# Output in two column halves, so that the left half of every block can be combined and stored under the last weight loads

## Chip, cores, metric

One core of one Trainium2 chip. The metric is the device time of one execution in microseconds, median of several. The trace's span is about 1.8 us shorter than the time, so spans are compared with spans and times with times.

## The reference, cut to what matters

Attention over 8 x 8 heads of 576 positions (a plain window of 32 in half of the heads, a dilated one in the other half), then a soft mixture of 8 experts with 4 slots each:

```python
x = attn_out.transpose(0, 2, 1, 3).reshape(4608, 512)
logits = x @ phi                           # (4608, 32)
d = softmax(logits, axis=0)                # dispatch: over all rows
slot_input = d.T @ x                       # needs every row
for e in range(8):
    slot_out[e] = relu(slot_input[e] @ w1[e]) @ w2[e]
c = softmax(logits, axis=1)                # combine
out = c @ slot_out                         # (4608, 512), fp32
```

An output element needs all 32 slots, so the slot outputs of all experts, so all of w2 — but only the columns of w2 that it lies in. That is what the change uses.

## The kernel before

All loads cast fp32 to fp16 on the way and are issued from POOL, as are the stores, which cast back. Weights stream in behind q, k, v through the whole kernel; w2 of experts 2, 3, 4, 6 and 7 comes last, into memory that the attention gives up.

```python
def load_w2(e, pieces=1):
    src = moe_w2[e].rearrange("(h p l) n -> p h (l n)", h=2, l=4)   # runs of 4 rows: 8 KB read, 4 KB written
    dst = w2t[e].rearrange("p (h l) n -> p h (l n)", h=2)
    if pieces == 1:
        nc.gpsimd.dma_start(out=dst, in_=src)
        return
    ...                                                             # expert 7 in four pieces
# order of the last loads: 0, 1, 5, 2, 3, 4, 6, then 7 in 4 pieces

so = psum_e.tile([128, DMODEL], FP32, name="so", tag="so")
early = [0, 1, 5, 2, 3, 4, 6]
jobs = [(e, 4 * fc + c) for fc in range(2) for e in early for c in range(4)]
jobs += [(7, c) for c in range(8)]
for i, (e, c) in enumerate(jobs):
    ...                                    # matmul: so[32a:32a+32, :] += h of expert e, times w2t[e][:, c, :]
nc.scalar.copy(out=so_sb[:, 0:256], in_=so[:, 0:256])
nc.vector.tensor_copy(out=so_sb[:, 256:512], in_=so[:, 256:512])
...
for blk in range(NFIN):                    # 36 blocks of 128 rows
    r0 = 128 * blk
    fp = psum_f.tile([128, DMODEL], FP32, name=f"f_{blk}", tag="f")
    nc.tensor.matmul(fp, ET[:, r0 : r0 + 128], so_sb, start=True, stop=True)
    ot = out_pool.tile([128, DMODEL], FP16, name=f"ot_{blk}", tag="ot")
    ...                                    # ACT and DVE in turn: ot = fp * rrow
    nc.gpsimd.dma_start(out=out[r0 : r0 + 128, :], in_=ot)
```

The softmax here doesn't subtract the row's maximum and nothing guards it: scores larger than these inputs give would overflow.

Of the kernel before, what the change touches and what calls it, by code (L numbers as in the profile page):

```python
# [9 lines left out]
FP32 = mybir.dt.float32  # L10
FP16 = mybir.dt.float16
U32 = mybir.dt.uint32
AF = mybir.ActivationFunctionType
ALU = mybir.AluOpType
# [10 lines left out]
DMODEL = H * D  # L25
# [14 lines left out]
NE = NT + DIL + 1  # L40
NFIN = N_ROWS // 128
UNITS = 7


def make_masks():
# [19 lines left out]
def kernel(  # L65
# [10 lines left out]
    nc = tc.nc  # L76
# [6 lines left out]
    consts = ctx.enter_context(tc.tile_pool(name="consts", bufs=1))  # L83
# [8 lines left out]
    ET = consts.tile([128, N_ROWS + 64], FP16, name="ET")  # L92
# [1 line left out]
    rcol = consts.tile([128, N_SLOTS], FP32, name="rcol")  # L94
    siTm = consts.tile([128, 4, E_EXP, N_SLOTS], FP16, name="siTm")
    rrow = consts.tile([128, NFIN], FP32, name="rrow")
    so_sb = consts.tile([128, DMODEL], FP16, name="so_sb")

    w1_pool = ctx.enter_context(tc.tile_pool(name="w1p", bufs=1))
    w2a_pool = ctx.enter_context(tc.tile_pool(name="w2a", bufs=1))  # L100
# [1 line left out]
    w2t = {e: w2a_pool.tile([128, 8, DMODEL], FP16, name=f"w2_{e}", tag=f"w2_{e}") for e in range(2)}  # L102
# [4 lines left out]
    QK_SLAB, V_SLAB = 2 * (32 + S + S + 80 + S + S + 16), 4096  # L107
    kTp, kTd, qTp, qTd, vP, vD, vL = [], [], [], [], [], [], []
    for i in range(2):
        slab = fix.tile([128, QK_SLAB], FP16, name=f"qk{i}", tag=f"qk{i}")  # L110
        o = 0
# [3 lines left out]
    for i in range(NV):  # L115
        slab = fix.tile([128, V_SLAB], FP16, name=f"v{i}", tag=f"v{i}")
        o = 0
# [4 lines left out]
    def slab_weights(e, tag, n):  # L122
        t = fix.tile([128, n], FP16, name=f"w2_{e}", tag=tag)
        w2t[e] = t[:, 0 : 8 * DMODEL].rearrange("p (c n) -> p c n", c=8)
# [5 lines left out]
    vs_pool = tc.alloc_tile_pool(name="vstage", bufs=2, side="right")  # L130
    raw_pool = tc.alloc_tile_pool(name="raw", bufs=2, side="right")
# [61 lines left out]
    def load_w1(e, i):  # L193
        src = moe_w1[e].rearrange("(c p) f -> p c f", p=128)
        nc.gpsimd.dma_start(out=w1t[e][:, 2 * i : 2 * i + 2, :], in_=src[:, 2 * i : 2 * i + 2, :])  # L195

    def load_w2(e, pieces=1):
        src = moe_w2[e].rearrange("(h p l) n -> p h (l n)", h=2, l=4)
        dst = w2t[e].rearrange("p (h l) n -> p h (l n)", h=2)
        if pieces == 1:  # L200
            nc.gpsimd.dma_start(out=dst, in_=src)
            return
        n = 8 * DMODEL // pieces
        for i in range(pieces):
            h, o = divmod(n * i, 4 * DMODEL)
            nc.gpsimd.dma_start(out=dst[:, h, o : o + n], in_=src[:, h, o : o + n])


    def qk_plain(ti, b):
# [69 lines left out]
    def emit_av(b, kind, i):  # L279
        u0, u1 = CHUNKS[kind][i : i + 2]  # L280
        o = psum_o.tile([128, UNITS, D + 1], FP32, name=f"o_{b}_{kind}{i}", tag="o")
        o_t[(b, kind, i)] = o
# [37 lines left out]
    def emit_norm(b, kind, i):  # L320
# [6 lines left out]
        else:  # L327
            if i == 0:
                xd_t[b] = x_pool.tile([128, DIL + 1, 4 * D], FP16, name=f"xd_{b}", tag="xd")
            x, nq = xd_t[b], 128  # L330
        rc = s_pool.tile([128, UNITS], FP32, name=f"rc_{b}_{kind}{i}", tag="rc")
        nc.vector.reciprocal(out=rc[0:nq, 0:n], in_=o[0:nq, 0:n, D])  # L332
# [127 lines left out]
    def weights(b, g):  # L460
        if b < B - 2:
            if g == 1 or b > 0:
                load_w1(*next_w1.pop(0))
        elif b == B - 2:
            if g == 0:
                while next_w1:
                    load_w1(*next_w1.pop(0))
                load_w2(0)
                load_w2(1)
            else:  # L470
                slab_weights(5, "v2", V_SLAB)
                load_w2(5)
        elif g == 0:
            nonlocal_pools["w2b"] = open_w2b()
        else:
            slab_weights(7, "v0", V_SLAB)
            load_w2(7, 4)

    nonlocal_pools = {}

    def open_w2b():
        raw_pool.release()
        vs_pool.release()
        pool = tc.alloc_tile_pool(name="w2b", bufs=1, side="right")
        for e in (2, 3, 4):
            w2t[e] = pool.tile([128, 8, DMODEL], FP16, name=f"w2_{e}", tag=f"w2_{e}")
            load_w2(e)
        slab_weights(6, "qk0", QK_SLAB)
        load_w2(6)
        return pool  # L490

    def slot0(b):
        att, b1, b2, b3 = b < B, b - 1 >= 0 and b <= B, 2 <= b < B + 2, b + 1 < B
        if att:
            qk_dil(1, b, 1)
            emit_scores(b, 0)
            if b + 2 < B:
                load_qk(0, b + 2)
                load_qk(1, b + 2)
            weights(b, 0)  # L500
# [28 lines left out]
    def slot1(b):  # L529
        att, b1, b3 = b < B, 1 <= b <= B, b + 1 < B  # L530
        if b3:
            qk_plain(0, b + 1)
        if att:
            emit_scores(b, 1)
            if b + 2 < B:
                load_v(b + 2)
            weights(b, 1)
            emit_av(b, "p", 0)
            emit_norm(b, "p", 0)
        if b1:  # L540
            back_xT_dil(b - 1, 0)
        if b3:
            qk_plain(1, b + 1)
        if att:
            emit_av(b, "p", 1)
            emit_norm(b, "p", 1)
        if b1:
            back_xT_dil(b - 1, 1)

    def slot2(b):  # L550
        att, b1, b3 = b < B, 1 <= b <= B, b + 1 < B
        if b3:
            qk_dil(0, b + 1, 0)
        if att:
            emit_scores(b, 2)
            emit_av(b, "p", 2)
            emit_norm(b, "p", 2)
        if b3:
            qk_dil(0, b + 1, 1)
        if b1:  # L560
            back_logits(b - 1, 0)
        if att:
            emit_av(b, "p", 3)
            emit_norm(b, "p", 3)
        if b3:
            qk_dil(1, b + 1, 0)
            spread_v_left(b + 1)
            shift_v_plain(b + 1)
            shift_v_left(b + 1)
        if b1:  # L570
            back_logits(b - 1, 1)

    with tc.manual_schedule(engines=None):
        prologue()
        for b in range(B + 2):
            slot0(b)
            slot1(b)
            slot2(b)
    w2b_pool = nonlocal_pools["w2b"]

    psum_o.release()
    psum_s.release()
# [2 lines left out]
    xT_pool.release()  # L585
    x_pool.release()
    h_pool = tc.alloc_tile_pool(name="hp", bufs=1)
    out_pool = tc.alloc_tile_pool(name="outp", bufs=10)


    psum_e = tc.alloc_tile_pool(name="psum_e", bufs=1, space=bass.MemoryType.PSUM)
    hTm = [h_pool.tile([128, 4, 128], FP16, name=f"hTm{g}", tag=f"hTm{g}") for g in range(4)]
    for g in range(4):
# [8 lines left out]
        out=diag,  # L602
        in0=UT[:, 0:4, :].rearrange("p c (e s) -> p c e s", e=E_EXP),
        in1=rcol.rearrange("p (e s) -> p e s", e=E_EXP)[:, None, :, :].broadcast_to(
            [128, 4, E_EXP, S_PER_E]
        ),
        op=ALU.mult,
    )
    hps = [psum_e.tile([128, 512], FP32, name=f"hps{fc}", tag=f"hps{fc}") for fc in range(2)]
    for fc in range(2):  # L610
        for g in range(2):
            for dc in range(4):
                for j in range(4):
                    e = 4 * g + j
# [4 lines left out]
                        start=(g == 0 and dc == 0),  # L619
                        stop=(g == 1 and dc == 3),  # L620
# [3 lines left out]
    for fc in range(2):  # L624
# [5 lines left out]
        for g in range(2):  # L630
            dst = hTm[2 * g + fc].rearrange("p c (j s) -> p c j s", j=4)[:, :, :, 16 * g : 16 * g + 16]
            (nc.vector.tensor_copy, nc.scalar.copy)[g](out=dst, in_=hT4[:, :, :, 16 * g : 16 * g + 16])
    rs = ring.tile([128, NFIN], FP32, name="rs", tag="ring")
    for blk in range(NFIN):
# [4 lines left out]
            start=True,  # L639
            stop=True,  # L640
        )
    nc.vector.reciprocal(out=rrow, in_=rs)
    so = psum_e.tile([128, DMODEL], FP32, name="so", tag="so")
    early = [0, 1, 5, 2, 3, 4, 6]
    jobs = [(e, 4 * fc + c) for fc in range(2) for e in early for c in range(4)]
    jobs += [(7, c) for c in range(8)]
    for i, (e, c) in enumerate(jobs):
        g, j, a = e // 4, e % 4, c % 4
        nc.tensor.matmul(  # L649
            so[32 * a : 32 * a + 32, :],  # L650
            hTm[2 * g + c // 4][:, c % 4, 32 * j : 32 * j + 32],
            w2t[e][:, c, :],
            start=(i < 4),
            stop=(i >= len(jobs) - 4),
        )
    nc.scalar.copy(out=so_sb[:, 0:256], in_=so[:, 0:256])
    nc.vector.tensor_copy(out=so_sb[:, 256:512], in_=so[:, 256:512])
    psum_e.release()


    psum_f = tc.alloc_tile_pool(name="psum_f", bufs=6, space=bass.MemoryType.PSUM)
    for blk in range(NFIN):
        r0 = 128 * blk
        fp = psum_f.tile([128, DMODEL], FP32, name=f"f_{blk}", tag="f")
        nc.tensor.matmul(fp, ET[:, r0 : r0 + 128], so_sb, start=True, stop=True)  # L665
        ot = out_pool.tile([128, DMODEL], FP16, name=f"ot_{blk}", tag="ot")
        if blk % 2 == 0:
            nc.scalar.activation(out=ot, in_=fp, func=AF.Copy, scale=rrow[:, blk : blk + 1])  # L668
        else:
            nc.vector.tensor_scalar(  # L670
                out=ot, in0=fp, scalar1=rrow[:, blk : blk + 1], scalar2=None, op0=ALU.mult
            )
        nc.gpsimd.dma_start(out=out[r0 : r0 + 128, :], in_=ot)  # L673
    psum_f.release()
    out_pool.release()
    h_pool.release()
    fix.release()
    w2b_pool.release()


# [28 lines left out]
```

## Time and profile before

| | before |
|---|---|
| time, median | 192.23 us (192.01 to 192.81) |
| span of the trace | 190.7 us |
| last w2 landing / first store landing / last store landing | 159.45 / 164.5 / 187.3 us |
| HBM read / written | 62.20 MB / 9.44 MB |

The landings are the issue times of the POOL timeline plus the landing time of each issue. The slices, the chain, the windows over the hole and the POOL timeline are shown in the prediction, which reads them.

### The profile page before, as it was taken

To read this page: it belongs to the slowest core of one execution; us is meant where nothing else is said; L and a number is where in the kernel's file an instruction comes from. 1 tells how busy PE (TensorE), PEld (TensorE's weight loads), DVE (VectorE), ACT (ScalarE), POOL (GpSimd) and SP (SyncE) were. 2 spreads that over 40 slices of the span, in tenths; PEclk is the share of its full clock that TensorE was granted. 3 is DMA by queue.
4 is the path that set the end of the run, shared out by engine and by line. 5 is a ranking of instruction groups with operands and counts; after the bars stand their busy time and mean duration, and the time that the engine had idled before them with its cause. 6 is when DMAs were issued, how large, how long until landed. Compare 5 with 4: busy or idle time off the path is not lost.

```text
span 190.7 us, 5116 instructions
## 1 busy us (share of the span) xinstructions
PE 127.4 (67%) x2224; PEld 72.1 (38%) x2224; DVE 104.5 (55%) x230; ACT 85.3 (45%) x144; POOL 96.2 (50%) x134
## 2 busy tenths in 40 slices
PE   2061058999996897894798799996960156878300
PEld 0031025757665365473357366555320022211000
DVE  3583708798999289689089794714120002756510
ACT  2031056777972764960764966540020002754500
POOL 7759762966944845834944662111100000998830
PEclk9999999999999699999589999955596558965555
DMA  5999999999999999999999999999999980999991
GB/s 122 182 181 205 189 200 194 210 197 195 214 198 197 215 195 202 210 194 203 210 195 201 211 212 214 217 211 217 215 213 218 208 161 13 303 407 407 410 405 50
DMA packets 40662, 41.00 MB, mean 215 GB/s; under 512 B 20800, under 2 KB 25536, under 8 KB 40640
## 3 DMA queue, kind: packets, MB, share of 16 engines
q0 software_dynamic: 40352, 40.41, 119.2%
q8 instruction: 17, 0.28, 0.5%
q1 hardware_dynamic: 288, 0.27, 0.5%
q14 instruction: 5, 0.04, 0.1%
HBM read 62.20 MB, written 9.44 MB: 376 GB/s over the span
## 4 chain that ended last, share of the span: by engine, by line
DMA 61%; PE 12%; issue 9%; POOL 7%; DVE 4%; ACT 3%; POOLq 0%; ACTq 0%
DMA w<-in_moe_w_dram 42%; DMA vsa<-in_v_dram 15%; DMA raw<-in_q_dram 4%; POOL out_dram L673 3%; ACT p L271 2%; PE sa L260 2%; PE sb L249 2%; PE lg L379 2%; POOL v L159 2%; DVE ot L670 2%; PE sa L249 1%; PE o_p L311 1%; PE o_d L311 1%; PE rd L360 1%; DVE qk L222 1%
## 5 line engine op out<-in xcount | busy, mean ns | idle before, releaser
L673 POOL DMA_DIRECT2D out_dram<-ot x36 | 19.0, 533 | 29.6 <-ACT ot L668 27.6
L271 ACT ACTIVATE p<-sa 128x576 f16<-128x576 f32 (+2 forms) x24 | 19.6, 818 | 20.0 <-PE sb L260 19.8
L249 PE MATMUL sa<-masks,ident 128*128 128x288 f16 (+2 forms) x48 | 14.5, 388 | 21.1 <-ACT p L271 17.6
L213 DVE STREAM_TRANSPOSE qk<-raw 128x576 uint32<-128x576 uint32 x16 | 20.0, 1250 | 8.1 <-DMA raw<-in_q_dram 6.7
L311 PEld LDWEIGHTS <-p 128*128 128x128 f16 (+2 forms) x448 | 17.5, 105 | 14.2 <-issue 9.2
L249 PEld LDWEIGHTS <-ident 128*128 128x128 f16 x96 | 9.8, 109 | 32.8 <-issue 27.3
L222 DVE STREAM_TRANSPOSE qk<-raw 128x320 uint32<-128x320 uint32 (+1 forms) x32 | 21.6, 679 | 0.3
L175 ACT COPY v<-vsa 128x1024 f16<-128x1024 f16 x8 | 8.4, 1045 | 25.2 <-DMA vsa<-in_v_dram 25.2
L271 ACT ACTIVATE p<-sb 128x576 f16<-128x576 f32 (+2 forms) x24 | 19.5, 813 | 0.0
L260 PE MATMUL sa<-qk 32*128 32x96 f16 (+2 forms) x448 | 16.1, 214 | 4.8 <-DVE qk L213 4.8
L333 DVE TENSOR_TENSOR xp<-o_p,rc_p 96x384 f16<-96x384 f32 x32 | 17.7, 554 | 1.3
L379 PE MATMUL lg<-xTd,phi 128*128 128x288 f16 x32 | 18.2, 659 | 0.0
L260 PEld LDWEIGHTS <-qk 32*128 32x128 f16 x896 | 12.5, 101 | 15.0 <-issue 9.5
L332 DVE RECIPROCAL rc_p<-o_p 96x6 f32<-96x6 f32 x32 | 5.7, 179 | 22.0 <-PE o_p L311 21.5
L670 DVE TENSOR_SCALAR ot<-f,rrow 128x512 f16<-128x512 f32 x18 | 13.1, 749 | 7.8 <-DMA out_dram<-ot 7.1
L665 PE MATMUL f<-so_sb,ET 128*128 128x512 f16 x36 | 14.8, 464 | 3.7 <-DVE ot L670 1.6
L311 PE MATMUL o_p<-v,p 128*128 128x65 f16 (+1 forms) x192 | 13.1, 211 | 5.1 <-POOL v L191 5.1
L260 PE MATMUL sb<-qk 32*128 32x96 f16 (+2 forms) x448 | 16.2, 214 | 0.0
L668 ACT ACTIVATE ot<-f,rrow 128x512 f16<-128x512 f32 x18 | 11.9, 689 | 8.7 <-PE f L665 4.8
L649 PE MATMUL so<-w,hTm 128*32 128x512 f16 x64 | 7.1, 536 | 12.8 <-DMA w<-in_moe_w_dram 12.4
L333 DVE TENSOR_TENSOR xd<-o_d,rc_d 128x448 f16<-128x448 f32 (+1 forms) x24 | 14.5, 602 | 0.8
L195 POOL DMA_DIRECT2D w<-in_moe_w_dram x16 | 11.4, 712 | 6.9 <-DMA raw<-in_k_dram 3.2
(77 smaller groups left out, 235.0 us busy)
## 6 DMA issues: line engine op xcount, KB each, us to landing
out_dram<-ot POOLq DMA_DIRECT2D x36, 256.0 KB, 4.5
w<-in_moe_w_dram POOLq DMA_DIRECT2D x16, 512.0 KB, 15.6
w<-in_moe_w_dram POOLq DMA_DIRECT2D x7, 1024.0 KB, 26.6
raw<-in_q_dram POOLq DMA_DIRECT2D x7, 576.0 KB, 12.5
raw<-in_k_dram POOLq DMA_DIRECT2D x7, 576.0 KB, 13.9
v<-in_v_dram POOLq DMA_DIRECT2D x8, 288.0 KB, 13.4
vsa<-in_v_dram POOLq DMA_DIRECT2D x8, 256.0 KB, 13.4
w<-in_moe_w_dram POOLq DMA_DIRECT2D x4, 256.0 KB, 30.9
```

Source lines behind the costliest of these rows:

```text
L213: nc.vector.transpose(out=dst, in_=src)
L222: nc.vector.transpose(out=o, in_=i)
L249: nc.tensor.matmul(sps[h // 2][:, h % 2, 0:n], ident, bias, start=True, stop=False, skip_group_check=True,)
L260: nc.tensor.matmul(sps[h // 2][:, h % 2, c0 : c0 + w], kt_[32 * h : 32 * h + 32, k0 : k0 + 128, tt], qt_[32 * h : 32 * h + 32, q0 : q0 + w ...
L271: nc.scalar.activation(out=pt, in_=sps[ab][:, :, 0:n], func=AF.Exp, scale=SCALE)
L311: nc.tensor.matmul(o[p0 : p0 + np_, n, :], l, rr, start=(k == 0), stop=(k == len(jobs) - 1), skip_group_check=True,)
L333: nc.vector.tensor_tensor(out=x.rearrange("p t (h d) -> p (t h) d", h=4)[0:nq, u0:u1, :], in0=o[0:nq, 0:n, 0:D], in1=rc[0:nq, 0:n, None].b ...
L379: nc.tensor.matmul(lp, phi4[:, kc].rearrange("p c s -> p (c s)"), rhs, start=(kc == 0), stop=(kc == 3))
L665: nc.tensor.matmul(fp, ET[:, r0 : r0 + 128], so_sb, start=True, stop=True)
L668: nc.scalar.activation(out=ot, in_=fp, func=AF.Copy, scale=rrow[:, blk : blk + 1])
L670: nc.vector.tensor_scalar(out=ot, in0=fp, scalar1=rrow[:, blk : blk + 1], scalar2=None, op0=ALU.mult)
L673: nc.gpsimd.dma_start(out=out[r0 : r0 + 128, :], in_=ot)
```

## The change

Intent: load w2 of the last four experts (3, 4, 6, 7) as left column halves first and right halves after all of those; then the left half of the slot outputs is complete while the right halves still load, and the left half of all 36 output blocks can be combined, evicted and put into the queue under those loads. Cut to its core:

```diff
-    def load_w2(e, pieces=1):
+    def load_w2(e, half=None):
...
+        src = moe_w2[e].rearrange("(h p l) n -> h p l n", h=2, l=4)
+        c0 = NH * half                                    # NH = 256
+        for h in range(2):
+            nc.gpsimd.dma_start(
+                out=w2t[e][:, 4 * h : 4 * h + 4, c0 : c0 + NH], in_=src[h][:, :, c0 : c0 + NH]
+            )
...
+            load_w2(2)
+            for e in HALVED[:3]:
+                load_w2(e, 0)
         else:
             slab_weights(7, "v0", V_SLAB)
-            load_w2(7, 4)
+            load_w2(7, 0)
+            for e in HALVED:
+                load_w2(e, 1)
+    HALVED = (3, 4, 6, 7)
...
-    for blk in range(NFIN):
+    def combine(half, pair):                              # two blocks of 128 rows, half the columns
+        fp = psum_f.tile([128, 2, NH], FP32, name=f"f{half}_{pair}", tag="f")
...
+        nc.gpsimd.dma_start(
+            out=out[r0 : r0 + 256, NH * half : NH * half + NH].rearrange("(k p) n -> p k n", k=2),
+            in_=ot,
+        )
+    with tc.manual_schedule(engines=None):
+        slot_out(0, ORDER)
+        slot_out(1, ORDER[:4])
+        at = {5: 0, 9: 1, 13: 2}
+        for pair in range(NFIN // 2):
+            combine(0, pair)
+            if pair in at:
+                slot_out(1, (HALVED[at[pair]],))
+        slot_out(1, HALVED[3:])
+        for pair in range(NFIN // 2):
+            combine(1, pair)
```

More of the change, by code (lines that the diff above doesn't have):

```diff
@@ L42 @@
 UNITS = 7
+NH = DMODEL // 2
 def make_masks():
@@ L96 @@
     rrow = consts.tile([128, NFIN], FP32, name="rrow")
-    so_sb = consts.tile([128, DMODEL], FP16, name="so_sb")
+    so_sb = [consts.tile([128, NH], FP16, name=f"so_sb{i}") for i in range(2)]
     w1_pool = ctx.enter_context(tc.tile_pool(name="w1p", bufs=1))
@@ L195, in load_w1 @@
         nc.gpsimd.dma_start(out=w1t[e][:, 2 * i : 2 * i + 2, :], in_=src[:, 2 * i : 2 * i + 2, :])
-    def load_w2(e, pieces=1):
-        src = moe_w2[e].rearrange("(h p l) n -> p h (l n)", h=2, l=4)
-        dst = w2t[e].rearrange("p (h l) n -> p h (l n)", h=2)
-        if pieces == 1:
-            nc.gpsimd.dma_start(out=dst, in_=src)
-            return
-        n = 8 * DMODEL // pieces
-        for i in range(pieces):
-            h, o = divmod(n * i, 4 * DMODEL)
-            nc.gpsimd.dma_start(out=dst[:, h, o : o + n], in_=src[:, h, o : o + n])
+    def load_w2(e, half=None):
+        if half is None:
+            nc.gpsimd.dma_start(
+                out=w2t[e].rearrange("p (h l) n -> p h (l n)", h=2),
+                in_=moe_w2[e].rearrange("(h p l) n -> p h (l n)", h=2, l=4),
+            )
+            return
+        src = moe_w2[e].rearrange("(h p l) n -> h p l n", h=2, l=4)
[4 more added lines that the diff above has]
+            )
     def qk_plain(ti, b):
@@ L473, in weights @@
         elif g == 0:
-            nonlocal_pools["w2b"] = open_w2b()
+            raw_pool.release()
+            vs_pool.release()
+            pool = tc.alloc_tile_pool(name="w2b", bufs=1, side="right")
+            late_pools.append(pool)
+            for e in (2, 3, 4):
+                w2t[e] = pool.tile([128, 8, DMODEL], FP16, name=f"w2_{e}", tag=f"w2_{e}")
+            slab_weights(6, "qk0", QK_SLAB)
+            load_w2(2)
+            for e in HALVED[:3]:
+                load_w2(e, 0)
         else:
             slab_weights(7, "v0", V_SLAB)
-            load_w2(7, 4)
-    nonlocal_pools = {}
-    def open_w2b():
-        raw_pool.release()
-        vs_pool.release()
-        pool = tc.alloc_tile_pool(name="w2b", bufs=1, side="right")
-        for e in (2, 3, 4):
-            w2t[e] = pool.tile([128, 8, DMODEL], FP16, name=f"w2_{e}", tag=f"w2_{e}")
-            load_w2(e)
-        slab_weights(6, "qk0", QK_SLAB)
-        load_w2(6)
-        return pool
+            load_w2(7, 0)
+            for e in HALVED:
+                load_w2(e, 1)
+    HALVED = (3, 4, 6, 7)
+    late_pools = []
     def slot0(b):
@@ L578 @@
             slot2(b)
-    w2b_pool = nonlocal_pools["w2b"]
     psum_o.release()
@@ L587 @@
     h_pool = tc.alloc_tile_pool(name="hp", bufs=1)
-    out_pool = tc.alloc_tile_pool(name="outp", bufs=10)
+    out_pool = tc.alloc_tile_pool(name="outp", bufs=NFIN // 2 + 6)
+    psum_so = tc.alloc_tile_pool(name="psum_so", bufs=1, space=bass.MemoryType.PSUM)
     psum_e = tc.alloc_tile_pool(name="psum_e", bufs=1, space=bass.MemoryType.PSUM)
@@ L642 @@
     nc.vector.reciprocal(out=rrow, in_=rs)
-    so = psum_e.tile([128, DMODEL], FP32, name="so", tag="so")
-    early = [0, 1, 5, 2, 3, 4, 6]
-    jobs = [(e, 4 * fc + c) for fc in range(2) for e in early for c in range(4)]
-    jobs += [(7, c) for c in range(8)]
-    for i, (e, c) in enumerate(jobs):
-        g, j, a = e // 4, e % 4, c % 4
-        nc.tensor.matmul(
-            so[32 * a : 32 * a + 32, :],
-            hTm[2 * g + c // 4][:, c % 4, 32 * j : 32 * j + 32],
-            w2t[e][:, c, :],
-            start=(i < 4),
-            stop=(i >= len(jobs) - 4),
-        )
@@ L656 @@
-    nc.scalar.copy(out=so_sb[:, 0:256], in_=so[:, 0:256])
-    nc.vector.tensor_copy(out=so_sb[:, 256:512], in_=so[:, 256:512])
-    psum_e.release()
-    psum_f = tc.alloc_tile_pool(name="psum_f", bufs=6, space=bass.MemoryType.PSUM)
-    for blk in range(NFIN):
-        r0 = 128 * blk
-        fp = psum_f.tile([128, DMODEL], FP32, name=f"f_{blk}", tag="f")
-        nc.tensor.matmul(fp, ET[:, r0 : r0 + 128], so_sb, start=True, stop=True)
-        ot = out_pool.tile([128, DMODEL], FP16, name=f"ot_{blk}", tag="ot")
-        if blk % 2 == 0:
-            nc.scalar.activation(out=ot, in_=fp, func=AF.Copy, scale=rrow[:, blk : blk + 1])
-        else:
-            nc.vector.tensor_scalar(
-                out=ot, in0=fp, scalar1=rrow[:, blk : blk + 1], scalar2=None, op0=ALU.mult
-            )
-        nc.gpsimd.dma_start(out=out[r0 : r0 + 128, :], in_=ot)
+    psum_e.release()
@@ new lines, with slot_out @@
+    so = [psum_so.tile([128, NH], FP32, name=f"so{i}", tag=f"so{i}") for i in range(2)]
+    ORDER = (0, 1, 5, 2) + HALVED
+    def slot_out(half, experts):
+        for e in experts:
+            for c in range(8):
+                g, j, a = e // 4, e % 4, c % 4
+                nc.tensor.matmul(
+                    so[half][32 * a : 32 * a + 32, :],
+                    hTm[2 * g + c // 4][:, c % 4, 32 * j : 32 * j + 32],
+                    w2t[e][:, c, NH * half : NH * half + NH],
+                    start=(e == ORDER[0] and c < 4),
+                    stop=(e == ORDER[-1] and c >= 4),
+                )
+        if experts[-1] == ORDER[-1]:
+            nc.scalar.copy(out=so_sb[half], in_=so[half])
@@ new lines @@
+    psum_f = tc.alloc_tile_pool(name="psum_f", bufs=4, space=bass.MemoryType.PSUM)
+    def combine(half, pair):
+        fp = psum_f.tile([128, 2, NH], FP32, name=f"f{half}_{pair}", tag="f")
+        r0 = 256 * pair
+        for k in range(2):
+            nc.tensor.matmul(
+                fp[:, k, :],
+                ET[:, r0 + 128 * k : r0 + 128 * k + 128],
+                so_sb[half],
+                start=True,
+                stop=True,
+                skip_group_check=True,
+            )
+        ot = out_pool.tile([128, 2, NH], FP16, name=f"ot{half}_{pair}", tag="ot")
+        if pair % 2 == 0:
+            for k in range(2):
+                blk = 2 * pair + k
+                nc.scalar.activation(
+                    out=ot[:, k, :], in_=fp[:, k, :], func=AF.Copy, scale=rrow[:, blk : blk + 1]
+                )
+        else:
+            nc.vector.tensor_tensor(
+                out=ot,
+                in0=fp,
+                in1=rrow[:, 2 * pair : 2 * pair + 2, None].broadcast_to([128, 2, NH]),
+                op=ALU.mult,
+            )
+        nc.gpsimd.dma_start(
+            out=out[r0 : r0 + 256, NH * half : NH * half + NH].rearrange("(k p) n -> p k n", k=2),
+            in_=ot,
+        )
@@ L674 @@
+    with tc.manual_schedule(engines=None):
[9 more added lines that the diff above has]
+            combine(1, pair)
     psum_f.release()
+    psum_so.release()
     out_pool.release()
@@ L677 @@
     fix.release()
-    w2b_pool.release()
+    late_pools[0].release()
 _INS = ['q', 'k', 'v', 'moe_phi', 'moe_w1', 'moe_w2']
```

## The prediction

> **What bounds the kernel now.** I read the page's slices first, to see which engine is full and when. Time before is 192.23 us, the profiled span 190.7, so one slice is 4.77 us.
>
> ```profile
> DMA  5999999999999999999999999999999980999991
> GB/s 122 182 181 205 189 200 194 210 197 195 214 198 197 215 195 202 210 194 203 210 195 201 211 212 214 217 211 217 215 213 218 208 161 13 303 407 407 410 405 50
> ```
>
> The DMA engines are full everywhere but in slices 33 to 35 (counted from 1) and at the end. A load is counted at its fp16 size, so 215 GB/s is 430 GB/s read from HBM; a store writes fp32, at 407. PE, DVE, ACT and POOL all have idle tenths throughout. So the kernel is bound by transfers, and what can be won is the hole between the last load and the first store. The chain of waits, in order of time, says what stands in it:
>
> ```profile
> 107.20 26.57 DMA w<-in_moe_w_dram
> 133.76 0.28 issue
> 134.05 25.41 DMA w<-in_moe_w_dram
> ...
> 159.50 0.41 PE so L649 x2
> 159.93 0.38 ACT so_sb L656
> 160.33 0.44 DVE so_sb L657
> ```
>
> The last piece of w2 lands at 159.45 us; then come the last slot-output matmuls, two copies, the first combine matmul and evictions, all before a byte of output can leave. Windows over the hole, where the last two columns are the mean busy share of the DMA engines and GB/s (about 1.06 is a full load, 1.47 a full store):
>
> ```profile
> 153.00:154.00 1.00, 0.00 (x0) 0.00 (x0) 0.00 (x0) 0.00 (x0) 0.00 (x0) 0.50 1.12 211
> 155.00:156.00 1.00, 1.00 (x16) 0.41 (x12) 0.00 (x0) 0.00 (x0) 0.00 (x0) 0.50 0.70 129
> 157.00:158.00 1.00, 1.00 (x16) 0.50 (x9) 0.00 (x0) 0.00 (x0) 0.00 (x0) 0.50 0.41 76
> 158.00:159.00 1.00, 0.71 (x10) 0.10 (x3) 0.00 (x0) 0.00 (x0) 0.00 (x0) 0.83 0.07 12
> 163.00:163.50 0.50, 0.50 (x2) 0.10 (x1) 0.50 (x2) 0.50 (x2) 0.50 (x2) 1.00 0.49 152
> 163.50:164.00 0.50, 0.30 (x2) 0.18 (x2) 0.50 (x2) 0.50 (x2) 0.50 (x2) 1.00 1.45 401
> ```
>
> Summed against 211 GB/s (409 for stores), about 6.8 us of mean DMA time is lost from 154 to 163.2 us. But the rate does not fall at once: it thins out over four microseconds, while the four quarters of the last expert land at 155.7, 157.0, 158.2 and 159.4 us (issue plus landing time, issue by issue). 1.25 us per quarter is the full pace (a whole expert takes 4.9 us, so 1.22). So some of the 16 engines finish early, and the slowest runs at full pace to 159.4. For the slowest engine the hole is only about 159.3 to 163.2.
>
> The POOL timeline shows a second rule:
>
> ```profile
> 124.27 0.54 POOL L206 DMA_DIRECT2D w<-in_moe_w_dram  x1 [4.10 <-DMA w<-in_moe_w_dram]
> 129.18 0.53 POOL L206 DMA_DIRECT2D w<-in_moe_w_dram  x1 [4.37 <-DMA w<-in_moe_w_dram]
> 134.05 0.53 POOL L206 DMA_DIRECT2D w<-in_moe_w_dram  x1 [4.33 <-DMA w<-in_moe_w_dram]
> ```
>
> Each issue waits for a landing: the one at 134.05 for the transfer issued at 107.20, eight issues earlier; the others fit the same count. So at most eight transfers of POOL are in flight.
>
> **What the Trainium skill says.** All four places are in "DMA: Bandwidth & Descriptors".
> 1. Section "Two DMAs through the same engine are not ordered": within one queue of one DMA engine, descriptors start in order. So stores issued behind the w2 loads don't take bandwidth from them; they follow. The trace agrees: landings come in issue order throughout.
> 2. Section "Why a DMA increments its semaphore by 16 and not by 1": only when all 16 engines have posted has the data landed. So the slowest engine sets every landing, as read above.
> 3. Section "Latency and other measured facts": two of the engines are usually slower than the rest. The views don't tell the engines apart, but the thinning tail of 155 to 159 us agrees with a few lagging ones.
> 4. Section "Why small descriptors are slow (HBM only)": a fixed cost of about 3 cycles for each packet and 32 bytes of descriptors. The trace has a case of the new size: vsa loads have 512-byte runs in SBUF, 256 KB in all, and landed 1.0 to 1.4 us after the transfer before them, mean of eight 1.275, against 1.22 for 256 KB of w2 in 4 KB runs. So the cost is there, at about 4%.
>
> **The change part by part.**
>
> *Loads.* Experts 3, 4, 6 and 7 are fetched as left halves and, after all of those, right halves: 16 transfers of 256 KB in 512-byte runs in place of 3 of 1 MB and 4 of 256 KB in 4 KB runs. Bytes are equal. At 1.275 instead of 1.22 each: 16 x 0.055 = 0.9 us later for the last landing, which is on the path. POOL issues cost about 0.76 us each (vsa's), below the 1.275 us that each takes on the wire, and eight in flight are 10 us of work: no starvation.
>
> *Left half under the loads.* The last left piece lands eight transfers, 10.2 us, before the last right piece. After that PE has 8 matmuls for expert 7 and 32 for the right half of four experts, at half width: 38 of full width took 4.22 us at half clock, so 40 half ones take 2.2 us. First combine at about -8 us, first store issued at -7. A pair costs ACT two 128x256 evictions (0.37 to 0.41 each, from the so_sb copy and half of 0.69 plus overhead), or DVE one 128x512 (about 0.7): both engines together a pair in 0.4 us; PE, two matmuls, 0.45. 18 pairs plus the slot matmuls between them end near +0.5 us. Stores 0 to 7 wait each for load 8 to 15 to land, so about seven stand in the queue when the last load ends: the engines go straight on.
>
> *Right half.* Matmuls of expert 7 (0.6), copy (0.4), combine and eviction (1): ready at about +2.5 us. It is first needed after 18 stores of 0.65 us less eight in flight, about +7. So it is hidden, with 4 us to spare.
>
> *Stores.* 36 transfers of 256 KB as before, but in 1 KB runs, not 2 KB. Before, the first landed at 164.5 and the last at about 187.27 (182.67 + 4.6): 22.77 / 35 = 0.651 each. vsa's extra 0.055 us is for 28 more packets per engine, 2 ns each; 8 more packets per engine make 0.016 a store, 0.6 us for 36. POOL's issue of a 256-run transfer cost 0.70 us (the w2 loads), above the 0.65 of the store, so POOL slowly eats the backlog: 28 issues after the last load, 19.7 + 0.7 us, then one transfer and its landing, some 2.3 us: +22.7. The wire needs 36 x 0.667 = 24.0. Just not the bound.
>
> *Sum.* From the last load's landing to the first store's: 159.45 to 164.5, 5.05 us; back to back it would be 0.65. Removed: 4.4 us. Added: 0.9 (loads), 0.6 (stores), 0.2 for POOL's small margin. Net -2.7 us: 192.23 - 2.7 = **189.5 us**, 1.4% faster. The tail after the last landing stays.
>
> **The rivals.**
> A. *The whole mean hole is won*: 6.8 - 1.5 = 5.3, 186.9 us, over 2%. It needs the slow engines to catch up during the stores. For it: the stores' end is sharp (369 GB/s at 186 to 186.5, then 25), so there they are nearly equal. Against: equal pace keeps a lag, it doesn't remove it, and the engine that finishes loading at 159.4 has all its stores still to do.
> B. *Small runs cost more than vsa tells.* Half rows lie 1 KB in every 2 KB of HBM, vsa's source doesn't skip. With 10% on the loads (2 us) and 5% on the stores (1.2), the gain is 4.4 - 3.2 = 1.2: 191.0 us. For it: the skill's overhead of 3 cycles in 32 or so for 1 KB is 9%. Against: vsa's measured 4%.
> C. *POOL becomes the bound of the stores.* If an issue takes 0.8 us, 28 x 0.8 + 3 = 25.4 against 24.0: 1.4 us given back, about 190.9. For: 0.70 is already over 0.65. Against: today's store issue is 0.53.
> D. *A late left half* (PE in program order, stuck on a right load) would open the hole again: 192 or more. Estimated slack is 7 us; unlikely.
>
> **Range and chances.** B and C together give some 191.5; half of A's excess and no packet cost give 187.7. Range 187.6 to 191.5. Faster by over 2% means under 188.4: it needs most of the packet cost gone, or part of A: 0.26. Slower by over 2% (196.1) needs B, C and D together: 0.02.
>
> **What would show it right or wrong.** Right: no slice under 8 tenths of DMA between the first and last; last w2 landing near 160.4; first store landing 0.6 to 0.8 us after it; 0.66 to 0.68 us from store to store; POOL's store issues near 0.70 us. A half load landing every 1.275 us confirms the load term; 1.35 or more is rival B. POOL busy without a pause while store latency falls below 3 us is C. A last store landing that spreads over 4 us of falling rate, as the loads do now, confirms the slow engine; a sharp end with a time under 188 is A. The prediction is wrong if stores displace loads, so that the last w2 piece lands well after 161.

## The result, and the profile after

The changed kernel took 189.95 us (189.2 to 190.53, four runs), before 192.12 in the same rounds; ratio 0.9882, 95% interval 0.9835 to 0.9929. Run again later, in other rounds: 189.5 us, ratio 0.9864 (0.9837 to 0.9890). A ratio is the mean time of one kernel's fast runs over that of the other's of the same rounds, so not quite the ratio of the medians quoted. The change is worth 1.2 to 1.4%, inside 2%, and clearly not zero.

The slices of the changed kernel, one being 4.72 us; they answer to the two lines that open the prediction:

```profile
DMA  5999999999999999999999999999999999999991
GB/s 113 188 180 207 189 202 192 213 200 195 213 202 192 214 201 185 210 202 185 212 202 194 212 212 214 216 214 214 209 196 198 194 196 266 331 364 378 378 383 24
```

The hole is gone: no slice between first and last is under nine tenths. Two things in the GB/s row are new. Where w2 halves load (slices 30 to 33) it reads 194 to 198 instead of 208 to 218, and where the stores run it reads 378 to 383 instead of 405 to 410. Both are the price of shorter runs, or of the way that the stores are issued.

The end of the chain of waits, in order of time:

```profile
151.18 10.42 DMA w<-in_moe_w_dram
...
161.63 0.49 issue
162.12 0.27 POOL out_dram L695
162.39 0.50 issue
162.88 5.27 DMA out_dram<-ot
```

Before, the last load was followed by matmul, copy, copy, matmul, eviction; now it is followed by a store's issue. The chain is transfers and their issue to its end.

The POOL timeline of the changed kernel around the last loads, and the first combine:

```profile
151.18 0.74 POOL L208 DMA_DIRECT2D w<-in_moe_w_dram  x1 [0.59 <-DMA w<-in_moe_w_dram]
...
154.81 2.82 POOL L695 DMA_DIRECT2D out_dram<-ot  x4 [2.90 <-ACT ot L685]
...
158.16 0.70 POOL L695 DMA_DIRECT2D out_dram<-ot  x1 [0.53 <-ACT ot L685]
159.45 0.71 POOL L695 DMA_DIRECT2D out_dram<-ot  x1 [0.59 <-DVE ot L689]
160.80 0.70 POOL L695 DMA_DIRECT2D out_dram<-ot  x1 [0.63 <-ACT ot L685]
162.12 3.57 POOL L695 DMA_DIRECT2D out_dram<-ot  x5 [0.62 <-DMA w<-in_moe_w_dram]
```

The first store is issued 6.8 us before the last w2 piece lands at 161.6 (151.18 + 10.4). Stores 5, 6, 7 and 8 follow 1.3 us apart: that is the landing of a half load, for each waits for the transfer eight issues earlier. The idle time is put down to ACT and DVE, but their tiles had been ready (left-half evictions ran ahead). Seven stores stand in the queue when the last load lands, as predicted.

The steps of the way, from landings of single transfers in the two traces (last of the 16 engines):

| stretch | before | after | difference | predicted |
|---|---|---|---|---|
| start to landing of expert 2 | 138.66 | 139.76 | +1.10 | 0 |
| to the last w2 landing | 20.79 | 21.83 | +1.04 | +0.9 |
| to the first store landing | 5.05 | 0.75 | -4.30 | -4.4 |
| first to last store landing | 22.79 | 23.70 | +0.91 | +0.6, +0.2 for POOL |
| last store landing to end of span | 3.38 | 2.73 | -0.65 | 0 |
| span | 190.67 | 188.77 | -1.90 | -2.7 |

The first row is not the change: no transfer up to it differs in the code. The trace holds one landing per engine and transfer, and the fastest engine lands expert 2 at 135.44 to 135.47 us in the trace before, in this one and in a second one of the same kernel (experiment 6). The slowest lags by 3.2, 4.3 and 5.0 us in these three.

Two other rows mislead when read alone. The row of the loads mixes the cost of half loads with the growth of the lag, which was 1.1 us in the trace before and 0.4 in this one. On the engine that lands first the same stretch took 19.68 us before and 21.40 after: the half loads cost 1.7 us, not 1.0. And the last row is no chance. The end after the last store landing (called the tail below) took 3.38 us in each of the three traces with the old loads and the old stores (the kernel before, experiments 1 and 2), and 2.72 to 2.73 us in each of the three with the new loads and 36 stores (this one, experiments 3 and 6). So the tail belongs to the program. Its cause was not tested.

### The profile page after: what moved, and what is told of

It is laid out like the page before. It is cut to its first block, busy times and chain, and to the rows that moved or that the text cites. A ratio compares the mean times of both kernels' runs of the same rounds, so it can differ in the third digit from the quotient of the medians.

```text
span 188.8 us, 5331 instructions
## 1 busy us (share of the span) xinstructions
PE 124.4 (66%) x2324; PEld 76.7 (41%) x2324; DVE 102.8 (54%) x229; ACT 87.9 (47%) x163; POOL 110.1 (58%) x143
## 4 chain that ended last, share of the span: by engine, by line
DMA 67%; PE 10%; POOL 8%; issue 5%; DVE 4%; ACT 3%; POOLq 0%; ACTq 0%
DMA w<-in_moe_w_dram 36%; DMA vsa<-in_v_dram 15%; DMA v<-in_v_dram 8%; DMA out_dram<-ot 5%; POOL out_dram L695 4%; DMA raw<-in_q_dram 4%; ACT p L275 2%; PE sa L264 2%; PE sb L253 2%; PE lg L383 1%; DVE qk L226 1%; POOL v L160 1%; DVE xp L337 1%; PE sa L253 1%; PE o_d L315 1%
## 5 line engine op out<-in xcount | busy, mean ns | idle before, releaser
L695 POOL DMA_DIRECT2D out_dram<-ot x36 | 25.3, 708 | 5.7 <-ACT ot L685 4.5
L253 PE MATMUL sa<-masks,ident 128*128 128x288 f16 (+2 forms) x48 | 13.8, 375 | 22.0 <-ACT p L275 18.3
L208 POOL DMA_DIRECT2D w<-in_moe_w_dram x16 | 11.9, 742 | 26.6 <-DMA w<-in_moe_w_dram 22.2
L689 DVE TENSOR_TENSOR ot<-f,rrow 128x512 f16<-128x512 f32 x18 | 12.1, 690 | 16.7 <-PE f L673 15.6
L685 ACT ACTIVATE ot<-f,rrow 128x256 f16<-128x256 f32 x36 | 14.3, 476 | 3.5 <-PE f L673 3.1
L196 POOL DMA_DIRECT2D w<-in_moe_w_dram x16 | 11.3, 709 | 6.2 <-DMA raw<-in_k_dram 2.1
L160 POOL DMA_DIRECT2D v<-in_v_dram x8 | 9.6, 1198 | 8.8 <-PE o_p L315 5.7
```

Source lines behind the costliest of these rows:

```text
L208: nc.gpsimd.dma_start(out=w2t[e][:, 4 * h : 4 * h + 4, c0 : c0 + NH], in_=src[h][:, :, c0 : c0 + NH])
L253: nc.tensor.matmul(sps[h // 2][:, h % 2, 0:n], ident, bias, start=True, stop=False, skip_group_check=True,)
L685: nc.scalar.activation(out=ot[:, k, :], in_=fp[:, k, :], func=AF.Copy, scale=rrow[:, blk : blk + 1])
L689: nc.vector.tensor_tensor(out=ot, in0=fp, in1=rrow[:, 2 * pair : 2 * pair + 2, None].broadcast_to([128, 2, NH]), op=ALU.mult,)
L695: nc.gpsimd.dma_start(out=out[r0 : r0 + 256, NH * half : NH * half + NH].rearrange("(k p) n -> p k n", k=2), in_=ot,)
```

## The experiments

Each kernel below was timed in five rounds beside the kernel before.

### 1. The hole by itself, first try

```diff
-    jobs += [(7, c) for c in range(8)]
```

The kernel before, expert 7 left out of the slot outputs (a wrong result), all its loads kept.

> The kernel before, with expert 7 left out of the slot outputs (wrong result on purpose) while its w2 is still loaded in full: the stores no longer depend on the last load, nothing else changes. Theory of the prediction (the slowest DMA engine is full until the last landing, so only the 4.4 us between last landing and first store beyond one store's 0.65 are lost): 192.1 - 4.4 = 187.7 us. Rival A (the mean DMA time lost from 154 to 163.2 us is what counts, 6.8 us): 185.3 us. If stores displace loads instead of following them, the last w2 landing moves clearly later than in the kernel before; the prediction's theory says it stays at the same distance from the landing of expert 2 (20.7 us).

Measured: 190.64 us, ratio 0.9908 (0.9874 to 0.9943). Neither theory's number. The timeline of this run shows why: PE's order is by halves of the hidden dimension, so that 32 matmuls at half clock still waited for expert 6.

```profile
154.88 3.61 PE L648 MATMUL so<-w,hTm 128*32 128x512 f16 x32 [4.28 <-DMA w<-in_moe_w_dram]
...
161.02 11.84 POOL L672 DMA_DIRECT2D out_dram<-ot  x22 [25.61 <-ACT ot L667]
```

The interval from last load to first store landing fell from 5.05 to 3.46 us, 1.6 us less, and the time by 1.6 (192.27 to 190.64). This fits the rule, but doesn't tell it from rival A, since both holes shrank alike. So once more, better.

### 2. The hole by itself, second try

```diff
-    early = [0, 1, 5, 2, 3, 4, 6]
+    early = [0, 1, 5, 2, 3, 4]
...
-    jobs += [(7, c) for c in range(8)]
```

> The hole experiment again, because in the first one the stores were not free: 32 matmuls still stood between the landing of expert 6 and the first store, and the hole only shrank from 5.05 to 3.46 us (the time fell by 1.6). Now experts 6 and 7 are both left out of the slot outputs (wrong result on purpose), all loads and all stores as in the kernel before. Theory of the prediction: first store lands 0.65 us after the last load, 192.3 - 4.4 = 187.9 us. Rival A (mean DMA time of 6.8 us is won): 185.5 us, with the engines ending together. Store pace 0.65 us and last landings of the stores spread over some 4 us between fastest and slowest engine would speak for the first.

Measured: 187.65 us, ratio 0.9767 (0.9743 to 0.9791): -4.5 us. The first store lands 0.71 us after the last load, the stores 0.64 us apart. Loads aren't displaced: expert 2 to the last piece takes 19.7 us. (The kernel before took 20.8, of which one hiccup of 1 us; see the end.) Windows over the place where the hole was, with the share of the DMA engines and GB/s last:

```profile
155.00:156.00 1.00, 1.00 (x5) 0.29 (x3) 1.00 (x3) 1.00 (x3) 1.00 (x3) 1.00 0.74 150
156.00:157.00 1.00, 0.80 (x4) 0.29 (x3) 1.00 (x3) 0.78 (x2) 1.00 (x3) 1.00 1.32 315
...
159.00:160.00 1.00, 0.00 (x0) 0.00 (x0) 0.00 (x0) 0.00 (x0) 0.32 (x2) 1.00 1.47 408
```

The engines that finish their loads early go on with stores at once, and the slowest finishes its loads at 159.3 us and begins its own stores then. The mean DMA time of 6.8 us could not be had (rival A, 185.5 us); the last engine's 4.4 could, within the noise (4.0 to 4.9 us by the interval; 4.3 in the trace, from 5.05 to 0.71). This is the whole prize of the change, without its costs.

### 3. The loads of the change alone

The kernel before with `load_w2` and the load order of the change, and nothing else of it:

```diff
-            load_w2(7, 4)
+            load_w2(7, 0)
+            for e in HALVED:
+                load_w2(e, 1)
...
-            load_w2(e)
...
-        load_w2(6)
+        load_w2(2)
+        for e in HALVED[:3]:
+            load_w2(e, 0)
```

> The kernel before with only the loads of the change: experts 3, 4, 6, 7 in left halves, then right halves; slot outputs, combine and stores as before. The load term of the prediction was +0.9 us (16 x 0.055). The trace of the changed kernel shows about 1.33 us from one half load's landing to the next against 1.235, which would make +1.5: 193.6 us. Rival B (small runs cost 10%): +2.0, 194.1 us or more. If the half loads cost nothing by themselves and are slow in the changed kernel only because stores run beside them: 192.1 us and 1.22 to 1.25 us per half load.

Measured: 193.0 us, ratio 1.0039 (1.0009 to 1.0070): +0.75 us, between +0.2 and +1.3. In its trace a half load takes 1.33 us, as in the changed kernel, so no store is needed to make it slow. POOL's issues show the pace, for each waits for a landing:

```profile
140.41 0.74 POOL L208 DMA_DIRECT2D w<-in_moe_w_dram  x1 [0.65 <-DMA w<-in_moe_w_dram]
141.74 0.74 POOL L208 DMA_DIRECT2D w<-in_moe_w_dram  x1 [0.59 <-DMA w<-in_moe_w_dram]
```

The prediction took 1.275 from vsa, with 1.22 for 256 KB of whole experts (1.23 in longer stretches: 4.9 us for 1 MB): its difference was too small by nearly half. On the engine that lands first the sixteen take 21.40 us here too, 1.7 more than before, and 1.4 more on the last one (22.22 against 20.79). That the time rose by only 0.75 fits a tail that is 0.65 us shorter. So +0.9 agrees with the time, but not for the prediction's reason. Rival B's time of 194.1 us is out; its 10% for a half load is nearer to the 8.7% measured than the prediction's 4%. B blamed the half rows that are skipped in HBM. This run doesn't separate them from the short runs, but vsa's source skips nothing within a head, and the last three of its eight loads take 1.33 us on the first engine (median of the twelve traces): short runs seem to be enough.

### 4. The stores of the change alone

The kernel before, with 36 stores of two blocks by half the columns; slot outputs and loads as before.

```diff
-    for blk in range(NFIN):
+    for half in range(2):
+        for pair in range(NFIN // 2):
...
+            nc.gpsimd.dma_start(
+                out=out[r0 : r0 + 256, cols].rearrange("(k p) n -> p k n", k=2), in_=ot
+            )
```

> The kernel before with only the shape of the stores changed: 36 stores of two 128-row blocks by half the columns (left ones first), 1 KB runs; loads and slot outputs as before, so the hole stays. If only the longer time on the wire counts (0.66 to 0.667 instead of 0.651 us per store): +0.3 to +0.6, 192.4 to 192.7 us. If POOL's issue of 0.70 us is the pace (here the stores start with an empty queue, without the seven issued early in the changed kernel): last issue ends near 162.3 + 36 x 0.70 = 187.5, landing 2 us later, about 189.5 instead of 187.3: 194.1 us, with landings 0.70 us apart and a landing latency that stays near 2.3 us.

Measured: 193.9 us, ratio 1.0078 (1.0045 to 1.0111): +1.5 us. All 36 issues follow one another 0.70 us apart, and the time from issue to landing, the last line of the line view of these stores, never builds up (min, median, max):

```profile
L691 POOL DMA_DIRECT2D out_dram<-ot x36: 699/712/726, 162.3 to 186.8; - x36
...
DMA to landing us min/median/max: 2.5/2.6/3.2
```

So here POOL's issue is the pace (rival C), and from the first store landing to the last it takes 24.9 us instead of 22.8. (The tail is 1.6 us shorter than before, 1.78 us, so the time shows less than the stores lost.) A 256 KB store takes 0.65 us on the wire and 0.71 to issue once it has 256 runs instead of 128 (0.53 before). In the changed kernel the same issue costs the same, but there the last landing of a store stood between 7.5 and 3.8 us after its issue, falling all the way: the seven stores queued under the loads are a reserve that POOL eats up, and it lasts to the end.

### 5. The changed kernel with fewer, larger stores

```diff
+        if pair % 2 == 0:
+            quad[half] = out_pool.tile([128, 4, NH], FP16, name=f"ot{half}_{pair}", tag="ot")
...
+        if pair % 2 == 1:
+            r0 -= 256
             nc.gpsimd.dma_start(
-                out=out[r0 : r0 + 256, ...].rearrange("(k p) n -> p k n", k=2),
+                out=out[r0 : r0 + 512, ...].rearrange("(k p) n -> p k n", k=4),
```

> The changed kernel with stores of four blocks by half the columns (512 KB, 18 of them) instead of two (256 KB, 36): half the store issues on POOL, same runs and bytes. Theory of the prediction (the wire of the slowest engine sets the stores, POOL has a small margin): within 0.3 us of the changed kernel, 189.6 to 190.2 us. Rival C (POOL's issue pace sets the stores): faster by 1 us or more, 188.9 or less.

Measured: 189.14 us, ratio 0.9846 (0.9810 to 0.9883), beside 0.9882 and 0.9864 of the changed kernel: 0.4 to 0.7 us less, and the intervals overlap. POOL now spends 0.75 us on 512 KB, and stores still land 1.32 us apart, 0.66 per 256 KB. So POOL is not the bound of the changed kernel's stores; the wire at 1 KB runs is. From the last load to the last store landing it takes 24.3 us here and 24.5 and 24.0 in the two traces of the changed kernel, while the tail is 1.99 us instead of 2.73: the small gain has the size of the tail's difference, and none is shown for the larger stores themselves. What changes besides is how the engines end. Windows at the end of this run, then of the changed kernel, then of the one before:

```profile
180.00:181.00 1.00, 0.00 (x0) 0.00 (x0) 0.00 (x0) 0.00 (x0) 0.00 (x0) 0.50 1.69 337
182.00:183.00 1.00, 0.00 (x0) 0.00 (x0) 0.00 (x0) 0.00 (x0) 0.00 (x0) 0.50 0.79 157
184.00:185.00 1.00, 0.00 (x0) 0.00 (x0) 0.00 (x0) 0.00 (x0) 0.00 (x0) 0.50 0.18 35
```

```profile
183.00:184.00 1.00, 0.00 (x0) 0.00 (x0) 0.00 (x0) 0.00 (x0) 0.00 (x0) 0.50 1.89 384
184.00:185.00 1.00, 0.00 (x0) 0.00 (x0) 0.00 (x0) 0.00 (x0) 0.00 (x0) 0.50 0.63 120
185.00:186.00 1.00, 0.00 (x0) 0.00 (x0) 0.00 (x0) 0.00 (x0) 0.00 (x0) 0.50 0.09 16
```

```profile
185.00:186.00 1.00, 0.00 (x0) 0.00 (x0) 0.00 (x0) 0.00 (x0) 0.00 (x0) 0.50 1.45 402
186.00:187.00 1.00, 0.00 (x0) 0.00 (x0) 0.00 (x0) 0.00 (x0) 0.00 (x0) 0.50 0.74 197
```

With POOL out of the way the share thins out over four microseconds: the slowest engine carries its lag of the loads (4.2 us) through to the end (4.5). In the changed kernel the slowest engine catches up from 4.8 to 1.5 us, in two steps: stores 5 to 8 are issued only as the last loads land, 1.3 us apart, so that the fast engines wait and the lag falls to 3.1; after that they are held to POOL's 0.70 us, the slowest keeps its 0.66, and the lag falls to 1.5. Before, all started the stores together after the hole and ended together. This is the slow-engine account in three pictures, and it says where something is still to be had: at 182 us the mean share is less than half of what it was at 180 (0.79 against 1.69).

### 6. The changed kernel again

> The changed kernel once more, unaltered, so that it stands in the same rounds as the others: 189.6 to 190.2 us. If the time of its profiled run was bad luck by 0.6 us in the part that the change doesn't touch, the landing of expert 2 comes near 138.7 us as in the kernel before, not 139.8.

Measured: 189.5 us, quoted above. The guess about the profiled run missed: expert 2 lands at 140.5 us, later still, with a lag of 5.0 us. Loads from there on take 21.40 us, first store 0.74 after, stores 23.20: against the kernel before +0.6, -4.3 and +0.4.

### 7. Fewer experts in halves

```diff
-    HALVED = (3, 4, 6, 7)
+    HALVED = (6, 7)                       # experts 3 and 4 whole again; in the next run (7,)
...
-        slot_out(0, ORDER)
-        slot_out(1, ORDER[:4])
+        slot_out(0, ORDER[:-1])
+        slot_out(1, EARLY)                # right half of the whole experts
+        slot_out(0, ORDER[-1:])
```

with the stores of experiment 5.

> The changed kernel with stores of four blocks, and only experts 6 and 7 loaded in halves (8 half loads in place of 16); the slot outputs of the whole experts' right half are put ahead of the last left expert. Theory: only the load term changes, half of it comes back (8 x 0.09 = 0.75 us by the traces, 0.4 by the time of the loads alone), the left half is ready about 5.3 - 3 us ahead of the last load, still in time: 188.4 to 188.8 us, against 189.1 of four-block stores with four experts in halves. If the window under the loads is too short, the first store lands more than 1.5 us after the last load and nothing is gained.

Measured: 188.57 us, ratio 0.9817 (0.9794 to 0.9839), in the middle of what was expected (188.4 to 188.8). Its interval and that of the changed kernel in the same rounds (0.9837 to 0.9890) barely touch. Against four experts in halves with the same stores it is 0.6 us less; in the traces the loads take 0.9 us less on the first engine, and the tail is 0.3 shorter (1.70 us). The first store, 512 KB, landed 1.59 us after the last load, so some 0.3 us over its time on the wire. The second landed 2.38 us after the first instead of 1.32.

> The same with expert 7 alone in halves (4 half loads). Theory: the load term falls by 1.1 us (0.55 by the time of the loads alone) against four experts, but the last left piece lands only 2.7 us before the last load and a four-block store needs two combined pairs first (some 2.5 us and 1 us to start): first store 1.5 to 2.2 us after the last load, so 0.2 to 0.9 us of hole come back: 188.5 to 189.2 us, no better than two experts.

Measured: 190.81 us, ratio 0.9930 (0.9908 to 0.9952). Missed by 2 us: the first store landed 4.24 us after the last load, not 1.5 to 2.2. PE, in program order and at half clock, is part of the reason:

```profile
154.05 3.57 PE L659 MATMUL so<-w,hTm 128*32 128x256 f16 x72 [4.27 <-DMA w<-in_moe_w_dram]
...
160.06 5.17 POOL L704 DMA_DIRECT2D out_dram<-ot  x7 [25.04 <-DVE ot L696]
```

The 72 matmuls include all right halves of seven experts, left standing until expert 6 had landed and then put between the left half and its combine. They end at 157.62 us, 0.9 us after the last left piece (156.74). This is akin to the failure called D in the prediction, and made by the experiment's own order. But the larger part is elsewhere: from there to the first issue it took 2.4 us, about the 2.5 expected, and from issue to landing 3.54 us, where the expectation allowed 1 us to start and some 1.3 on the wire.

### 8. The same with PE's order mended

```diff
-        slot_out(0, ORDER[:-1])
-        slot_out(1, EARLY)
-        slot_out(0, ORDER[-1:])
+        for e in EARLY:
+            slot_out(0, (e,))
+            slot_out(1, (e,))
+        slot_out(0, HALVED)
```

and the first four stores with two blocks, the rest with four:

```diff
+        n = 2 if half == 0 and pair < 4 else 4
```

> Experts 6 and 7 alone in halves; the right half of the whole experts is multiplied right after their left half, as each lands (in the run before, 60 matmuls in a row held up the first combine); the first four stores have two blocks, all later ones four. Theory: with two experts in halves the first store landed 1.59 us after the last load because POOL got its first tile at 158.75; now the first store is issued about 2 us after the last left piece, 3.3 us ahead of the last load, so it lands 0.7 us after it: 0.9 us less, 188.6 - 0.9 = 187.7 us. If the last hole had another cause (the stores' issue, or the engines' order), no change: 188.6 us.

Measured: 188.95 us, ratio 0.9829 (0.9806 to 0.9853): not better than 188.57. The step aimed at was mended, the first store lands 0.72 us after the last load. The third store then lands 1.54 us after the second, on the slowest engine. That doesn't explain the missing gain, for the run before had such a delay too, of 1.06 us, at its second store. From the last load to the last store landing the trace is 0.5 us better (24.6 against 25.1); it loses 1.1 in the loads, where the lag grows by 1.0 us, and in the run before didn't grow. Whether the medians differ for that reason can't be told from one trace of each kernel; see also the last section.

> The same with expert 7 alone in halves: 0.4 us less of load cost than with two, but the last left piece lands only 2.7 us ahead of the last load; 2 us of chain and 1 us from issue to first bytes leave the first store landing 1.0 to 1.3 us after the last load: 187.6 to 188.0 us, equal to two experts in halves within the noise. With 4.24 us of hole in the last run of one expert, a fall of about 3 us is expected by the theory that only this interval counts.

Measured: 190.92 us, ratio 0.9940 (0.9920 to 0.9960). Missed by 3 us. The first store lands 2.76 us after the last load: the left chain took 2.74 us from landing (156.84) to the first issue (159.58), not 2, and issue to landing 2.65, not 1.7 (experiment 4 shows 2.5 to 2.6 for a store into an empty queue; the estimate had ignored it). Then the third store lands 2.97 us after the second: one of the 16 engines is 2.4 us behind all others. The theory that only the interval from the last load to the first store counts fails here. That interval is 1.5 us shorter than in the first run with one expert in halves (2.76 against 4.24), and the time is no less (190.92 against 190.81). Of the three windows tried, two half loads are too short, four and eight are not.

## Why the prediction was right

The call (189.5 us, within 2%) was right, and so was its mechanism: the hole went, by what the slowest engine lost in it. But two of its terms were off by 0.65 to 0.8 us in opposite directions, the loads and the tail, and that they nearly cancel is luck.

- **Transfers bound the kernel, and the hole counts by the slowest engine.** Right: experiment 2 gives 4.5 us for 4.4, and rival A's 6.8 is refuted. In the changed kernel the interval fell by 4.3.
- **Load term.** Too small by nearly half: +0.9 foreseen, +1.7 on the engine that lands first (21.40 against 19.68 us, the same in experiments 3 and 6). A half load takes 1.33, not 1.275 us, close to the 1.35 that the prediction named as the sign of rival B. The working took the mean of eight vsa loads, counted by last landings, which move when the lag does: 0.92 to 1.38 us by the trace (the prediction says 1.0 to 1.4), with 1.32 to 1.33 for the last three. The +1.04 in the table and the +0.75 in time are near 0.9 because of the lag and the tail.
- **The tail.** It was to stay, and fell by 0.65 us. This made up for most of the load term's miss.
- **The sign that stores displace loads.** The last w2 piece landed at 161.6 us, and at 161.9 in the second trace, after the 161 that the prediction named. They were not displaced: expert 2 had already landed 1.1 and 1.8 us late, and on the first engine the loads take the same 21.40 us without stores among them.
- **Left half ready in time.** First store issued at -6.8 us, foreseen -7; seven queued, foreseen seven.
- **Right half hidden.** Its first eviction is at 162.8, 1.2 us after the last load; its first store was not waited for.
- **Stores.** +0.4 to +0.9 in two traces, foreseen +0.6 and 0.2; 0.66 to 0.68 us each, foreseen 0.667. The issue at 0.70 us was met (708 ns), and the reserve of queued stores kept it off the path, as worked out; without the reserve the stores took 2.1 us longer, and the time rose by 1.5 (experiment 4).
- **The end of the stores.** The text expected four microseconds of thinning. Only 1.5 were seen, because the wait for landings and POOL's pace let the slowest engine catch up; with larger stores the four appear (experiment 5). The prediction had the facts, eight in flight, POOL's 0.70 and the engine's 0.667, and did not put them together.
- **Not foreseen.** The lag of the slowest engine at expert 2 varies from 3.2 to 5.0 us between traces. The spread of the changed kernel's times is of the same order (1.3 and 1.6 us); that the lag makes it is not shown, for at most two runs of a kernel were traced. The tail differs from kernel to kernel, from 3.38 us to 1.5 to 2.0 with four-block stores.
- **"A few lagging ones".** Of the 16 engines in the trace before, six land the last piece within 0.35 us of the first, the other ten 1.05 to 4.3 us later. So most lag.
- **A sum.** Rivals B and C together don't give 191.5 us: C's 25.4 us stands against B's slower stores of 24.6, which adds 0.8 to B's 191.0.

## What to carry to other kernels

Where sixteen engines share a transfer, measure a gap from the landing of the last piece, not from the mean rate: the mean counts time that a lagging engine does not have. Measure a cost per transfer, though, on the engine that lands first, for last landings also move with the lag. Work that is to fill a gap has to be queued before the gap, and its issue cost is then paid from the reserve; the same stores issued late are bound by the issuing engine. Splitting by columns halves the runs, so split no more than the window needs — but leave the window some 5 us here: two experts in halves did as well or better than four, one lost over half of the gain. Part of the small differences, here 0.3 to 1 us, can be a tail that has nothing to do with the reason for the change; so look at it in the trace before a gain is explained.

## What the Trainium skill lacked or had wrong

- "DMA: Bandwidth & Descriptors", section "Latency and other measured facts", says that two engines are usually slower. Here the last engine isn't slower at its pace (every quarter of expert 7 takes 1.25 us on the first and on the last engine alike); its lag came in steps, and ten of the 16 were over 1 us behind the first. In the trace before, it rose by 1.0 us at expert 4, while a 16 KB transfer of the queue "instruction" ran that took 0.95 us by itself on one engine. The DMA view of that stretch shows it:

```profile
DMA packets 111, 0.44 MB, mean 219 GB/s; under 512 B 7, under 2 KB 7, under 8 KB 110
...
q8 instruction: 1, 0.02, 3.0%
```

  There are 17 of these before and 18 after, where the program has more instructions; the 18th falls at 161 to 163 us in the changed kernel and in experiments 5 to 8, among the first stores. In the changed kernel's trace one store there landed 1.18 us after the one before it instead of 0.67. The point belongs to "Runtime: NRT & Kernel Launch", section "Instruction fetch mechanics", which describes fetches in blocks of this size, or to the DMA page; neither says what they take from the data. That these transfers are such fetches is read from the queue's name and their size. That they make the lag is inferred from times that fit, not tested: from 15 us on, the lag has three steps over 1 us in the trace before, each just after one of the 17, while the other 14 left none of that size. They don't explain all of the 2.97 us of the last experiment.
- The same page, "Why small descriptors are slow (HBM only)", gives a cost per packet. Sixteen loads of 256 KB (fp16) in 512-byte runs took 21.40 us on the first engine, the same bytes in 4 KB runs 19.68, so 8.7% and, with 28 more packets per engine, about 3.8 ns each. The 9% that rival B estimated from the page was nearer than the 4% read from vsa. For stores, 1 KB runs 0.66 against 0.65 with 2 KB.
- The same page, "Issuing engines are not separate DMA queues", calls the time to initiate a DMA "usually small relative to the DMA itself". From POOL it was 0.53 us for 128 runs, 0.71 for 256 and 0.74 for 512, against 0.65 us on the wire for a 256 KB store: with 256 runs, the issue was the bound (experiment 4).
- None of the pages read has the lag between the engines as a quantity: 3.2 to 5.0 us from run to run at the same point of this program, for the slowest of the 16, while the fastest repeated to 0.03 us in the three traces of the result section (135.2 to 136.3 us over all twelve).
